# A GpSimd drain ahead of the last scatters, full-height products for PV's last keys, and two standing x buffers

## The chip, the cores and the metric

The kernel runs on one NeuronCore of a Trainium2 chip. Its five engines each take instructions from a queue of their own, in order: TensorE (PE, with its weight loads as PEld), VectorE (DVE), ScalarE (ACT), GpSimd (POOL) and SyncE (SP), which mostly issues DMAs. GpSimd issues DMAs too, those whose rows are picked by an index. The metric is the device time of one execution in microseconds, the median of several runs.

## The reference

Three layers run one after the other, on 4 batches of 576 tokens and 512 features.

```
scores = q k^T / 8 - (cum_i - cum_j), causal;  cum = cumsum(max(s, 0))     8 heads of 64
x  = softmax(scores) v                                                     [4, 576, 512]
x  = (sigmoid(conv5(x)) * (x @ w_val)) @ w_out                             gated convolution
e  = the expert of each token: argmax(x @ w_gate) if local gate < 0.5, else the previous token's
out = softmax(x @ w_gate)[e] * relu(x @ w1[e]) @ w2[e]                     8 experts, 1024 wide
```

All inputs and outputs are float32.

## The kernel before

The first part of the program is the attention and the convolution layer, the second the experts.

Attention goes over 16 pairs of heads (`attention(p)`, 4 pairs for each batch). A pair's queries are cut into tiles of 128 and a rest of 64. For each tile PE makes the scores (L648, L653), where the bias comes in as one more product with gate rows `G`; DVE adds the mask and takes the row minimum (L680, L693), ACT takes the exponential (L701), POOL scales by the reciprocal sum (L725), PE transposes the result through a unit matrix (L737) and ACT or DVE copy it to the buffers `PT0` and `PT1` (L747 to L762). The 576 keys are four blocks of 128 and a last block of 64. The last block is transposed for both heads of the pair by L739 and copied by L755 into 64 partitions of `PT1`.

PV (`pv`, L789) then multiplies by v. It works on two halves of the queries: half 0 has 256 columns and keys 0 to 255, half 1 has 320 columns and all keys. The two heads lie side by side in the array, 64 columns each. The step for the last 64 keys (`j == 4`) takes its v from the tile `rv`, 64 partitions, loaded once for each batch by `last64`, and has K = 64. ACT copies the result into a tile `x` (L799) with four zero columns in front (L797, written on POOL), which the five taps of the convolution read (DVE, L814 and L816) and which POOL splits into a high and a low part (L803, L807). There are two x buffers; the first use of one is the s input.

What sets the order: every piece of work in the first part is a step with an engine, an estimated cost, what it waits for and a rank, and `Plan.order` simulates the engines and writes the instructions in the order that comes out. Buffers are taken into account as slots. A step's instructions are all issued where the step stands. POOL's first steps are constants: the unit matrix, `gr_set`, `zeros` (L290), the masks, small ones and blanks. `bias_rows` makes the gate rows `gr` from s: DVE scans, POOL multiplies (L390), and SP writes them to DRAM as `gates` (L407). `bias_in` loads each pair's `G` (L590), the first pair's straight from `gr`.

The experts come in a loop (`ffn`), in the order of their load. `up(e)` makes the hidden layer (L1375 to L1382), `turn` transposes gathered token rows for the next expert, `down(e, h)` makes the output (L1549), and POOL scatters each block of rows to the output in DRAM (L1458). The last expert's last block is made and scattered in two halves (`down_end`, L1516 to L1526). POOL's gathers and scatters wait in its queue for their indices and rows. At the end all engines meet (L1663): SP waits for every landing, each engine executes DRAINs, and the semaphores are cleared.

The loop that the last part of the change touches is

```
for e in range(E):
    if 0 < e < E - 1:
        tokens(e + 1)
    h = up(e) if e else up_first()
    if e + 1 < E:
        turn(e + 1, 0)
        turn(e + 1, 1)
    down(e, h)
```

Of the kernel before, what the change touches and what calls it, by code (L numbers as in the profile page):

```python
# [8 lines left out]
F32 = mybir.dt.float32  # L9
# [11 lines left out]
B, H, S, D = 4, 8, 576, 64  # L21
# [154 lines left out]
def build(tc, q, k, v, s, w_val, conv_w, w_out, w_gate, w_local, w1, w2, out, dbg=None):  # L176
    nc = tc.nc
    with ExitStack() as ctx:
# [75 lines left out]
        HL = {"q": (1, 0, -0.125), "k": (2, 3, 1.0)}  # L254


        PT0 = ap_.tile([P, 2, 384], F32, name="PT0")
        PT1 = ap_.tile([P, 2, 4 * 320 + P], F32, name="PT1")
        ready = {}
# [19 lines left out]
        def constants():  # L279
# [8 lines left out]
                                            channel_multiplier=1)  # L288

            def zeros():  # L290
                for g in G:
                    nc.gpsimd.memset(fv(g), 0.0)
                for t in QK:
                    nc.gpsimd.memset(fv(t[0:64, 0:2, 576:640]), 0.0)
                    nc.gpsimd.memset(fv(t[64:P, 0:2, 512:576]), 0.0)
# [51 lines left out]
        def bias_rows():  # L347

            plan.rank = -8
            ss, sg, s1, sc = slot("x"), slot("gr"), slot("g"), slot("g")
            tl = {}

            def s_zero():
                tl["s"] = new(mp, "x", "s_sb", [48, S])
                nc.vector.memset(tl["s"], 0.0)

            def one_set():
                tl["one"] = new(mp, "g", "one", [48, S])  # L360
                nc.vector.memset(tl["one"], 1.0)

            def gr_set():
                gr = tl["gr"] = new(ap_, "gr", "gr", [48, 4, 2, 640], F32R)
                nc.gpsimd.memset(fv(gr[:, 0::2, 0]), 1.0)
                nc.gpsimd.memset(fv(gr[:, 1::2, 1]), 1.0)
                nc.gpsimd.memset(fv(gr[:, 0::2, 1, 576:640]), 0.0)
                nc.gpsimd.memset(fv(gr[0:16, :, 0, 576:640]), 0.0)
                nc.gpsimd.memset(fv(gr[32:48, :, 0, 512:576]), 0.0)

            def scan():
                s_sb, cum = tl["s"], new(mp, "g", "cum", [48, S])
                tl["cum"] = cum
                nc.vector.tensor_scalar(s_sb, s_sb, 0.0, None, ALU.max)
                nc.vector.tensor_tensor_scan(cum, tl["one"], s_sb, 0.0, ALU.mult, ALU.add)

            def keys(z):
                gr, cum = tl["gr"], tl["cum"]
                if z == 0:
                    nc.vector.tensor_scalar(gr[:, 0, 1, 0:S], cum, -1.0, None, ALU.mult)  # L380
                else:
                    nc.vector.scalar_tensor_tensor(gr[:, 2, 1, 0:S], cum, -1.0, fv(gr[:, 0, 1, 0:S]), ALU.mult,
                                                   ALU.subtract)

            def queries(z, on_pool):
                gr = tl["gr"]
                for a, e, i, o, n in ((0, 48, 0, 0, 512), (0, 16, 512, 512, 64), (32, 48, 512, 576, 64)):
                    src, dst = fv(gr[a:e, 2 * z, 1, i:i + n]), gr[a:e, 2 * z + 1, 0, o:o + n]
                    if on_pool:
                        nc.gpsimd.tensor_scalar(dst, src, -1.0, 1.0, ALU.mult, ALU.mult)  # L390
                    else:
                        nc.scalar.activation(dst, src, AF.Copy, scale=-1.0)

            a = add("DVE", 0.6, s_zero, on=[ss])
            d = [add("SP", 0.1, lambda h=h: nc.sync.dma_start(
                out=tl["s"][32 * h:32 * h + 16], in_=s.rearrange("b (p two) s -> two (b p) s", two=2)[h]), a, on=[ss],
                lat=FAR) for h in range(2)]
            o = add("DVE", 0.6, one_set, on=[s1])
            w = ready["gr_set"] = add("Pool", 2.6, gr_set, on=[sg])
            c = add("DVE", 1.1, scan, d, o, on=[ss, s1, sc])  # L400
            k, r = None, []
            for z in range(2):
                k = add("DVE", 0.68 if z else 0.4, lambda z=z: keys(z), c, w, k, on=[sc, sg])
                p = R["qP"] > z
                r.append(add(*(("Pool", 1.0) if p else ("ACT", 0.95)), lambda z=z, p=p: queries(z, p), k, on=[sg]))
            ready["gr"], ready["gr_slot"] = (tl, r), sg
            ready["gates"] = [add("SP", 0.91, lambda h=h: nc.sync.dma_start(  # L407
                out=gates[:, h].rearrange("p r k s -> p (r k) s"),
                in_=fv(tl["gr"][32 * h:32 * h + 16]).rearrange("p r k s -> p (r k) s")), r, on=[sg], rank=0.2, lat=FAR)
                for h in range(2)]  # L410
# [80 lines left out]
        def load(p, nm):  # L491
# [19 lines left out]
            if p % NP == 0:  # L511
                sr = rest[b, nm, "slot"] = slot("r" + nm)

                def last64():
                    t = rest[b, nm] = new(ap_, "r" + nm, f"r{nm}_{b}", [64, H, D])
                    nc.sync.dma_start(out=t, in_=src[b, :, 512:576].rearrange("h p d -> p h d"))
                rest[b, nm, "step"] = add("SP", 0.28, last64, on=[sr], lat=FAR)
            return steps, sn
# [79 lines left out]
        def attention(p):  # L598
# [121 lines left out]
            def weigh(u, i, ss, st_, r):  # L720
# [13 lines left out]
                def turn():  # L734
                    ps = tl["pt"] = ps_t.tile([P, 4, P], F32, tag="t", name=f"t_{p}_{u}")
                    for j in range(min(t + 1, 4)):
                        nc.tensor.transpose(ps[:, j], tl["tt"][:, P * j:P * j + P], ident)  # L737
                    if fifth:
                        nc.tensor.transpose(ps[0:64, 1], last4["tl"]["tt"][:, 512:576], ident)  # L739

                def far(h, c, w, n):
                    return PT1[:, h, 0:1280].rearrange("p (j s) -> p j s", s=320)[:, 0:n, c:c + w]
# [9 lines left out]
                        nc.scalar.activation(far(0, 256, 64, 4), ps[:, :, 0:64], AF.Copy)  # L752

                def ev5():
                    nc.scalar.activation(PT1[0:64, :, 1344:1408], tl["pt"][0:64, 1].rearrange("j (h i) -> j h i", h=2),  # L755
                                         AF.Copy)
                half = 0 if t < 2 else 1
                a = add("PE", 0.107 * (min(t + 1, 4) + fifth), turn, n, last4["n"] if fifth else None,
# [18 lines left out]
            def pv(half):  # L777
                tl["ps", half] = ps_s.tile([P, 512], F32, tag="s", name=f"pv_{p}_{half}")
                vt, vr = nat[p]["v"], rest[b, "v"]
                for j in range(5) if half else range(2):  # L780
                    K = P if j < 4 else 64
                    if half:
                        c = (0, 0, 0, P, 256)[j]
                        o = 320 * j + c if j < 4 else 1344
# [2 lines left out]
                        c, o, w = P * j, 2 * P * j, 256 - P * j  # L787
                    for h in range(2):
                        nc.tensor.matmul(tl["ps", half][64 * h:64 * h + 64, c:c + w],  # L789
                                         lhsT=vt[0:K, j, h] if j < 4 else vr[:, 2 * hp + h],  # L790
                                         rhs=(PT1 if half else PT0)[0:K, h, o:o + w], start=j == 0,
                                         stop=j == (4 if half else 1))

            def x_out(half):
                if "x" not in tl:
                    tl["x"] = new(mp, "x", f"x_{p}", [P, 4 + S])
                    nc.gpsimd.memset(tl["x"][:, 0:4], 0.0)  # L797
                w = 320 if half else 256
                nc.scalar.activation(tl["x"][:, 4 + 256 * half:4 + 256 * half + w], tl["ps", half][:, 0:w], AF.Copy)  # L799

# [510 lines left out]
        def ffn():  # L1311
# [261 lines left out]
            for e in range(E):  # L1573
# [3 lines left out]
                if e + 1 < E:  # L1577
                    turn(e + 1, 0)
                    turn(e + 1, 1)
                down(e, h)  # L1580


# [85 lines left out]
```

## Time and profile before

| | |
|---|---|
| median of 3 runs | 619.11 us (618.69 to 619.46) |
| profiled execution | 616.59 us, its span 614.8 us |
| mean granted clock of TensorE | 0.984 |
| PE busy | 577.8 us, 4346 matmuls |
| DVE busy | 410.5 us |
| ACT busy | 339.4 us |
| POOL busy | 243.7 us |
| attention and convolution | about the first 315 us |
| first and last PV product (L789) | 37.1 and 313.7 us |

The profile shows one execution. Its span runs from the first to the last instruction; the execution's own time has 1.8 us more around that. A busy share is an average over stages with different limits, so the stretches have to be looked at one by one. In the rows below, the times of a timeline's row are its start, its length, and in brackets how long the engine stood idle before it and what ended that. A q behind an engine's name (POOLq, SPq) is its queue's own instructions, which don't count as busy. A drain is one of these.

### The profile page before, as it was taken

Reading aid. Unit: us, or ns where it says so; the run is one execution under the profiler, and the core shown is the slowest. Engines: PE = TensorE matmul, PEld = TensorE weight load, DVE = VectorE, ACT = ScalarE, POOL = GpSimd, SP = SyncE. Lnnn points to the kernel's source line nnn. Section 1 sums busy time; section 2 is a strip of 40 time slices with the busy share of each in tenths; the row PEclk is TensorE's granted clock in tenths of the full one; section 3 lists DMA queues with packets and bytes.
Section 4 is the critical chain, followed back from the end, with each engine's and each line's share of the span. In section 5 each row is a group of like instructions: output and inputs, shape, how many; then the busy total and the mean of one; then the engine's idle time right before and its main releaser. Section 6 shows DMA issues by size and latency. Waiting matters only on the chain. (4 is left out here: it accounts for less than half of the span.)

```text
span 614.8 us, 12466 instructions
## 1 busy us (share of the span) xinstructions
PE 577.8 (94%) x4346; PEld 503.3 (82%) x4346; DVE 410.5 (67%) x1029; ACT 339.4 (55%) x869; POOL 243.7 (40%) x377
## 2 busy tenths in 40 slices
PE   5899989999899988999989989999999999999994
PEld 4677678778777887777979987898998999999894
DVE  5589999968887668886699356455353636465550
ACT  2669868787478953677334325544243536355440
POOL 8367868553543433464550344030404004033101
PEclk8989999999999998999999999999999999999997
DMA  7734322322132310210133725273645537365710
GB/s 163 130 92 144 91 81 77 86 55 64 46 87 64 81 47 27 63 28 29 26 125 136 139 59 164 79 245 111 196 171 171 190 107 253 104 244 171 263 47 29
DMA packets 82838, 68.96 MB, mean 112 GB/s; under 512 B 60557, under 2 KB 66829, under 8 KB 82740
## 3 DMA queue, kind: packets, MB, share of 16 engines
q1 hardware_dynamic: 78788, 58.24, 33.2%
q0 software_dynamic: 3984, 9.88, 4.8%
q8 instruction: 36, 0.59, 0.4%
q14 instruction: 30, 0.25, 0.2%
HBM read 57.90 MB, written 10.79 MB: 112 GB/s over the span
## 5 line engine op out<-in xcount | busy, mean ns | idle before, releaser
L725 POOL TENSOR_SCALAR tt<-tt,st 128x512 f32<-128x512 f32 (+2 forms) x144 | 93.0, 661 | 103.0 <-DVE st L714 52.0
L1308 DVE TENSOR_TENSOR wl<-raw,wh 128x1024 fp32r<-128x1024 f32 x64 | 78.3, 1224 | 34.2 <-ACT wh L1305 33.8
L701 ACT ACTIVATE tt<-tt,st 128x384 f32<-128x384 f32 (+3 forms) x144 | 83.2, 583 | 12.4 <-DVE st L680 8.6
L1375 PE MATMUL h<-xth,wh 128*128 128x256 f32 (+5 forms) x256 | 73.7, 306 | 1.4 <-DVE xtl L1115 1.4
L1375 PE MATMUL h<-xth,wl 128*128 128x256 f32 (+5 forms) x256 | 72.9, 302 | 0.0
L680 DVE CUSTOM_DVE_ANT_0 tt<-s,mask 128x512 f32<-128x512 f32 (+3 forms) x128 | 57.9, 483 | 13.9 <-PE s L653 7.5
L1458 POOL DMA_INDIRECT out_dram<-out,id x21 | 28.6, 1362 | 96.7 <-ACT out L1456 83.3
L1305 ACT ACTIVATE wh<-raw 128x1024 fp32r<-128x1024 f32 x64 | 66.5, 1052 | 0.3 <-DMA raw<-in_moe_w_dram 0.3
L816 DVE SCALAR_TENSOR_TENSOR g<-x,cw,g 128x576 f32<-128x576 f32 x64 | 64.8, 1012 | 0.7
L737 PE MATMUL t<-ident,tt 128*128 128x128 f32 x384 | 61.9, 283 | 3.5 <-POOL tt L725 2.2
L1381 ACT ACTIVATE hh<-h 128x256 fp32r<-128x256 f32 (+5 forms) x64 | 27.1, 425 | 58.5 <-PE h L1375 52.1
L1382 DVE SCALAR_TENSOR_TENSOR hl<-h,hh 128x256 fp32r<-128x256 f32 (+5 forms) x64 | 29.8, 469 | 43.4 <-ACT hh L1381 43.4
L737 PEld LDWEIGHTS t<-ident,tt 128*128 128x128 f32 x384 | 43.3, 142 | 15.7 <-POOL tt L725 8.1
L1340 POOL DMA_INDIRECT xg<-x2d,id x20 | 20.9, 1046 | 87.2 <-DMA id<-ids 59.2
L929 PE MATMUL x<-wo_h,yl 128*128 128x266 f32 (+3 forms) x144 | 43.2, 300 | 7.8 <-DVE y L874 2.9
L653 PE MATMUL s<-QK 64*128 64x256 f32 (+2 forms) x384 | 48.9, 356 | 1.2 <-DVE st L693 1.2
L1375 PEld LDWEIGHTS h<-xth,wh 128*128 128x128 f32 x256 | 48.3, 189 | 1.9 <-DVE xtl L1115 1.6
L1375 PEld LDWEIGHTS h<-xth,wl 128*128 128x128 f32 x256 | 48.4, 189 | 0.2
L789 PE MATMUL pv<-PT,nv 128*64 128x320 f32 (+3 forms) x384 | 47.3, 386 | 0.0
L1375 PE MATMUL h<-xtl,wh 128*128 128x256 f32 (+5 forms) x256 | 46.3, 302 | 0.0
L929 PE MATMUL x<-wo_h,yh 128*128 128x266 f32 (+3 forms) x144 | 41.6, 289 | 0.0
L929 PE MATMUL x<-wo_l,yh 128*128 128x266 f32 (+3 forms) x144 | 41.6, 289 | 0.0
(269 smaller groups left out, 1499.4 us busy)
## 6 DMA issues: line engine op xcount, KB each, us to landing
raw<-in_moe_w_dram SPq DMA_DIRECT2D x64, 512.0 KB
nv<-in_v_dram SPq DMA_DIRECT2D x32, 128.0 KB
x2d<-x SPq DMA_DIRECT2D x32, 128.0 KB
nk<-in_k_dram SPq DMA_DIRECT2D x26, 128.0 KB
nq<-in_q_dram SPq DMA_DIRECT2D x26, 128.0 KB
wsc<-in_moe_w_val_dram SPq DMA_DIRECT2D x4, 512.0 KB
wsc<-in_moe_w_out_dram SPq DMA_DIRECT2D x4, 512.0 KB
nk<-in_k_dram SPq DMA_DIRECT2D x3, 256.0 KB
```

What stands on the lines that cost most here:

```text
L653: nc.tensor.matmul(ps[hh][:, 0:N], lhsT=q[:, P * t:P * t + P], rhs=k[:, 0:N], start=n == 0, stop=n == 3)
L680: nc.vector.tensor_tensor_reduce(out=tl["tt"][:, 0:W], in0=ps[h][:, 0:W], in1=mask[:, 512 - W:512], scale=1.0, scalar=3.0e38, op0=ALU.add, ...
L701: nc.scalar.activation(tt[:, 0:W], tt[:, 0:W], AF.Exp, bias=st[:, 0, i:i + 1], scale=-1.0, accum_out=st[:, 1, i:i + 1])
L725: nc.gpsimd.tensor_scalar(tl["tt"][:, 0:W], tl["tt"][:, 0:W], st_["st"][:, 2, i:i + 1], 1.0, ALU.mult, ALU.mult)
L737: nc.tensor.transpose(ps[:, j], tl["tt"][:, P * j:P * j + P], ident)
L789: nc.tensor.matmul(tl["ps", half][64 * h:64 * h + 64, c:c + w], lhsT=vt[0:K, j, h] if j < 4 else vr[:, 2 * hp + h], rhs=(PT1 if half else ...
L816: nc.vector.scalar_tensor_tensor(tl["g"], x[:, t:t + S], cw[:, hp, t:t + 1], tl["g"], ALU.mult, ALU.add)
L929: nc.tensor.matmul(ps[0:m, 0:c1 - c0], lhsT=yy[:, kc] if both else yy[:, kc, P * t:P * t + m], rhs=wt_[:, kc, c0:c1], start=n == 0, stop=n ...
L1305: nc.scalar.activation(hi, raw, AF.Copy)
L1308: nc.vector.tensor_tensor(lo, raw, fv(hi), ALU.subtract)
L1375: nc.tensor.matmul(ps[:, 0:N], lhsT=w[:, P * f:P * f + P], rhs=xx[:, kc, c], start=n == 0, stop=n == 11)
L1382: nc.vector.scalar_tensor_tensor(hl[:, c], ps[:, 0:N], 0.0, fv(hh[:, c]), ALU.max, ALU.subtract)
```

## The change

Four things are edited.

1. In the last expert, between `up` and `down`, POOL gets a `drain`.
2. The tile for the last 64 keys of v becomes `VR`, one standing tile with 128 partitions. The keys lie in partitions 64 to 127, the partitions 0 to 63 are set to zero once. L739 turns columns 448 to 575 of the last tile, where it had 512 to 575, so that 128 rows come out; the 64 ahead meet the zero rows. The copy to `PT1` is of 128 partitions, and all steps of PV have K = 128.
3. The x buffers are two standing tiles `X`. Their four zero columns are written once, in `zeros`, and the memset in `x_out` is gone.
4. `zeros` writes these two pads and VR's zero rows ahead of G and QK. Its planned cost stays the same, and so does the order of all other steps.

```
+        X = [mp.tile([P, 4 + S], F32, name=f"X{n}") for n in range(SIZES["x"])]
+        VR = ap_.tile([P, H, D], F32, name="VR")
...
             def zeros():
+                for x in X:
+                    nc.gpsimd.memset(x[:, 0:4], 0.0)
+                nc.gpsimd.memset(VR[0:64], 0.0)
                 for g in G:
                     nc.gpsimd.memset(fv(g), 0.0)
...
             def s_zero():
-                tl["s"] = new(mp, "x", "s_sb", [48, S])
+                tl["s"] = X[0][0:48, 4:4 + S]
...
                 def last64():
-                    t = rest[b, nm] = new(ap_, "r" + nm, f"r{nm}_{b}", [64, H, D])
+                    if nm == "v":
+                        rest[b, nm] = VR
+                        t = VR[64:P]
+                    else:
+                        t = rest[b, nm] = new(ap_, "r" + nm, f"r{nm}_{b}", [64, H, D])
...
                     if fifth:
-                        nc.tensor.transpose(ps[0:64, 1], last4["tl"]["tt"][:, 512:576], ident)
+                        nc.tensor.transpose(ps[:, 1], last4["tl"]["tt"][:, 448:576], ident)
...
                 def ev5():
-                    nc.scalar.activation(PT1[0:64, :, 1344:1408], tl["pt"][0:64, 1].rearrange("j (h i) -> j h i", h=2),
+                    nc.scalar.activation(PT1[:, :, 1344:1408], tl["pt"][:, 1].rearrange("j (h i) -> j h i", h=2),
                                          AF.Copy)
...
-                    K = P if j < 4 else 64
...
                         nc.tensor.matmul(tl["ps", half][64 * h:64 * h + 64, c:c + w],
-                                         lhsT=vt[0:K, j, h] if j < 4 else vr[:, 2 * hp + h],
-                                         rhs=(PT1 if half else PT0)[0:K, h, o:o + w], start=j == 0,
+                                         lhsT=vt[:, j, h] if j < 4 else vr[:, 2 * hp + h],
+                                         rhs=(PT1 if half else PT0)[:, h, o:o + w], start=j == 0,
                                          stop=j == (4 if half else 1))
...
             def x_out(half):
-                if "x" not in tl:
-                    tl["x"] = new(mp, "x", f"x_{p}", [P, 4 + S])
-                    nc.gpsimd.memset(tl["x"][:, 0:4], 0.0)
+                tl["x"] = X[(p + 1) % len(X)]
...
                 if e + 1 < E:
                     turn(e + 1, 0)
                     turn(e + 1, 1)
+                else:
+                    nc.gpsimd.drain()
                 down(e, h)
```

How the instructions stand now is shown at two places. The first is POOL's queue at the start of the program, from the last memsets of the gate rows `gr` to the mask, as it was before:

```order
L369 MEMSET gr 16x4x64
L292 MEMSET G_102 128x1280
L292 MEMSET G_103 128x1280
L294 MEMSET QK_104 64x2x64
L295 MEMSET QK_104 64x2x64
L294 MEMSET QK_105 64x2x64
L295 MEMSET QK_105 64x2x64
L281 MEMSET mask 128x512
```

And the same place of the changed kernel:

```order
L374 MEMSET gr 16x4x64
L294 MEMSET X_106 128x4
L294 MEMSET X_107 128x4
L295 MEMSET VR 64x512
L297 MEMSET G_102 128x1280
L297 MEMSET G_103 128x1280
L299 MEMSET QK_104 64x2x64
L300 MEMSET QK_104 64x2x64
L299 MEMSET QK_105 64x2x64
L300 MEMSET QK_105 64x2x64
L283 MEMSET mask 128x512
```

Three memsets have come in ahead of G; everything behind stands as it did.

The second is PE's queue at the PV of pair 0, where `nv` holds v's first 512 keys and `rv` or `VR` the last 64. Before:

```order
L789 MATMUL pv_0_627<-PT_106,nv_196 64x256 x2
L789 MATMUL pv_0_627<-PT_106,nv_196 64x128 x2
L789 MATMUL pv_1_637<-PT_107,nv_196 64x320 x6
L789 MATMUL pv_1_637<-PT_107,nv_196 64x192 x2
L789 MATMUL pv_1_637<-PT_107,rv_216 64x64 x2
L648 MATMUL s_4_1_658<-QK_105 128x288 x3
```

And in the changed kernel:

```order
L797 MATMUL pv_0_631<-PT_109,nv_198 64x256 x2
L797 MATMUL pv_0_631<-PT_109,nv_198 64x128 x2
L797 MATMUL pv_1_641<-PT_110,nv_198 64x320 x6
L797 MATMUL pv_1_641<-PT_110,nv_198 64x192 x2
L797 MATMUL pv_1_641<-PT_110,VR 64x64 x2
L657 MATMUL s_4_1_660<-QK_105 128x288 x3
```

No instruction of PE has moved; the last step reads another tile, with 128 rows. On POOL the 16 memsets of the x tiles are gone from their places. The drain is not listed in such rows; it stands behind the scatters of expert 6.

## Rows read from the trace of the kernel before

**Rows 1.** The page: busy us, share of the span, instructions.

```profile
PE 577.8 (94%) x4346; PEld 503.3 (82%) x4346; DVE 410.5 (67%) x1029; ACT 339.4 (55%) x869; POOL 243.7 (40%) x377
```

**Rows 2.** Stretches: length, busy us of the five engines, clock, DMA share, GB/s.

```profile
80.00:120.00 40.00, 38.68 (x331) 30.69 (x330) 38.90 (x110) 29.41 (x92) 27.26 (x34) 1.00 0.35 90
240.00:280.00 40.00, 39.35 (x319) 30.59 (x320) 30.89 (x96) 26.24 (x80) 19.96 (x33) 0.96 0.19 48
```

**Rows 3.** Instructions of L1663: ns min/median/max, first and last start us.

```profile
L1663 POOLq DRAIN  x3: 46/103/5462, 608.5 to 614.5; - x3
L1663 SPq DRAIN  x3: 7/7/13, 609.7 to 614.2; - x3
```

**Rows 4.** Timeline of POOL, the last expert's scatters.

```profile
601.27 0.98 POOL L1458 DMA_INDIRECT out_dram<-out,id  x1 [15.88 <-ACT out L1456]
...
606.80 0.98 POOL L1526 DMA_INDIRECT out_dram<-out,halves  x1 [1.81 <-POOLq L1223]
```

**Rows 5.** DMA issues of POOL's queue: count, median us to landing.

```profile
xg<-x2d,id POOLq DMA_INDIRECT x22, 3.7
out_dram<-out,id POOLq DMA_INDIRECT x21, 5.8
ids<-tokp,place POOLq DMA_INDIRECT x20, 4.4
```

**Rows 6.** Instructions of L1652, the program's start.

```profile
L1652 POOLq DRAIN  x1: 186/186/186, 0.3 to 0.3; - x1
```

**Rows 7.** Timeline of POOL, 4 to 15 us.

```profile
4.34 2.27 POOL L292 MEMSET G<- 128x1280 f32 x2
...
7.52 0.53 POOL L281 MEMSET mask<- 128x512 f32 x1
...
12.96 1.64 POOL L390 TENSOR_SCALAR gr<-gr 48x512 fp32r<-48x512 f32 x3
```

**Rows 8.** Timeline of SP's queue and of PE, gate rows of pairs 0 and 1.

```profile
16.10 1.45 SPq L590 DMA_DIRECT2D G<-gr  x2
...
27.19 0.87 SPq L590 DMA_DIRECT2D G<-gates  x2
...
30.74 0.77 PE L653 MATMUL s<-G 64*128 64x512 f32 x2 [2.25 <-DMA G<-gates]
```

**Rows 9.** Timeline of PE in three instants: what runs then, pair 15's PV.

```profile
313.16 0.50 PE L789 MATMUL pv<-PT,nv 128*64 128x192 f32 x4
...
313.32 0.33 PE L789 MATMUL pv<-PT,nv 128*64 128x192 f32 x2
313.58 0.27 PE L789 MATMUL pv<-PT,rv 64*64 64x64 f32 x2
...
313.69 0.22 PE L789 MATMUL pv<-PT,rv 64*64 64x64 f32 x2
313.85 0.39 PE L929 MATMUL x<-wo_h,yl 128*128 128x266 f32 x1
```

**Rows 10.** Instructions that read rv, and idle time ahead of them (us, times).

```profile
L789 PE MATMUL pv<-PT,rv x64: 218/242/268, 39.9 to 313.7; 64*64 64x64 f32 x64
...
  issue: 3.3, 12
```

**Rows 11.** Instructions of L739 and L737.

```profile
L739 PE MATMUL t<-ident,tt x16: 271/272/273, 35.5 to 307.6; 128*64 128x128 f32 x16
...
L737 PE MATMUL t<-ident,tt x384: 270/273/469, 24.8 to 309.2; 128*128 128x128 f32 x192
```

**Rows 12.** Instructions of L797, and who waited for them (us, times).

```profile
L797 POOL MEMSET x<- x16: 93/98/422, 36.2 to 311.5; 128x4 f32 x16
...
  PEld t L737: 0.2, 1
```

**Rows 13.** Timeline of PE at 238.89.

```profile
238.89 0.39 PE L929 MATMUL x<-wo_h,yl 128*128 128x266 f32 x1 [2.93 <-DVE y L874]
```

**Rows 14.** The stretch behind it, columns as in group 2.

```profile
239.80:243.00 3.20, 3.20 (x16) 3.20 (x16) 2.63 (x7) 0.87 (x2) 0.31 (x1) 0.50 0.11 39
```

## The prediction

> **What bounds the kernel now.** I read the page's busy shares first: TensorE (PE) is busy 94% of a span of 614.8 us [rows 1]. Then I cut the attention part into stretches. From 240 to 280 us PE is busy 39.35 of 40 us and leads alone; from 80 to 120 us VectorE (DVE) is as full as PE, 38.90 against 38.68 of 40 us [rows 2]. So microseconds taken from PE count in full in the later stretches, and only in part where DVE is level with it. Last I read the two ends, where PE isn't the bound. The instructions of the program's last line show what fills the end: GpSimd (POOL) executes three DRAINs of 46, 103 and 5462 ns, the first from 608.5 us on; SyncE (SP), which collects all landings, starts its own at 609.7 [rows 3]. So from about 609.8 to 614.0 the chip waits for one POOL instruction, 4.2 us. At the front POOL works through its constants without a pause, and the gate rows of the first attention pair wait for it [rows 7, 8].
>
> **The drain.** The new instruction stands on POOL behind the scatters of expert 6 and ahead of those of the last expert, the first of which starts at 601.27 after 15.88 us idle [rows 4]. A drain of even 5.5 us lies wholly inside that, and nothing but that scatter is queued behind it. What is the last drain worth if an earlier one has done its work? The trace has four POOL drains: 186 ns at the start, ahead of any DMA from this queue [rows 6], then the long one behind some 63 of them (22 + 21 + 20 [rows 5]; three others leave the quotient the same within 5%), then the two short ones with none in between. Which of the three in the group is the long one follows from the times: it starts at 608.5, and the last at 614.5. So a drain's length goes with what was issued since the one before. 5462 / 63 is 87 ns per DMA. With a drain near 585 us, three scatters are left for the last one (601.27, one in between, 606.80 [rows 4]): 3 x 87 ns = 0.26 us, or 0.45 with the 186 ns of an empty one. It would end before 609.1, ahead of SP. SP is late next, and the end moves from 614.0 to 609.8: **-4.2 us**. The bounds are 0 (the long time is a fixed price of any DMA since the last drain; 3 cost as much as 66) and -4.2 (SP's row). I take -4.2: the rows at hand range with the work behind them.
>
> **PV's last 64 keys.** PV runs two column halves of 64 side by side, and every product comes as two passes, so a step is two pairs of records. Before, the last step uses 64 rows (64\*64) behind steps of 128 rows (128\*64). At pair 15 the last two 192-column pairs start at 313.16 and 313.32, 0.16 us apart; the 64-row pair behind starts at 313.58, 0.26 later [rows 9]. So 0.10 us go where the shape of the array changes. The weight loads say the same: 3.3 us of "issue" (waiting for nothing that shows) ahead of them in 12 places [rows 10]. With 128 rows there is no change of shape at the entry: 64 products [rows 10] are 16 steps of four, 16 x 0.10 = 1.6 us less. The exit: 0.16 us from the second 64-row pair (313.69) to the next instruction (313.85) [rows 9]. In 7 of the 16 steps, by the order of PE, the next is PV's other half with the shape 128\*64, and 0.16 becomes the 0.11 of unbroken pairs (313.58 to 313.69): 7 x 0.05 = 0.35. Together 1.9 us. Inside the step I leave the spacing at 0.11, the row of this very step; if the wider shape hides the weight loads it could halve, 16 x 0.055 and 7 x 0.055 more, 3.2 in all. The transpose in front (L739) loads 64 columns of weights and gets 128; it takes 272 ns and the 128-wide ones a median of 273 [rows 11]. So it costs nothing, nor does its eviction, which has as many elements in each partition as before.
> How much reaches the end: ten of the 16 steps lie behind 120 us, where PE leads; of the six before I count half, so 13/16 of 1.9, 1.5; I take **-1.4 us**, between -3.2 and 0 (all of it lost in waits for DVE).
>
> **The buffers.** 16 memsets of 128x4 with a median of 98 ns leave POOL, 1.6 us. The list of who waited for them has one entry, PE's weight loads for 0.2 us [rows 12]: **-0.2**, between -1.6 and 0. What replaces them stands at the front, ahead of the G memsets: two of 128x4 and one of 64x512, for which the nearest row is mask's, 128x512 in 0.53 us [rows 7]. With the small ones between 0 (overlapped) and 98 ns each that is 0.53 to 0.73 us. From there POOL has no pause: even the multiplications of gr, which feed the gates, start at 12.96 without an idle time [rows 7], so they end 0.6 later. Queued behind them: SP waits for them with G<-gr at 16.10, and in SP's queue behind that stand nk, both gates stores, nq and the loads G<-gates at 27.19, for which PE stands idle 2.25 us, until 30.74 [rows 8]. PE's first gate products wait for the same. So **+0.6 us**, between 0 (what SP issues in between swallows it) and +0.73.
>
> **The sum.** -4.2 - 1.4 - 0.2 + 0.6 = -5.2 us on the profiled execution's 616.59, so 611.4. The median of the runs is 619.11, 2.5 above that execution; I carry the 2.5 over: 613.9 us.
>
> **Rivals.**
> 1. The drain has a fixed price. Then the new one costs 5.5 us in POOL's idle time and the last one 5.5 again. For it: there is only one long drain in the trace, so "per DMA" and "once" can't be told apart by it. Against it: it runs 4.2 us past the point where SP has seen every landing, so it isn't waiting for data, and what outlasts the data is more likely bookkeeping that grows with the DMAs. It gives -1.0: 618.1.
> 2. The gain on PE is lost in waits for DVE, which is 97% busy from 80 to 120 us and also ends PE's 2.93 us wait at 238.89 [rows 2, 13]. Only the late start, the memsets and the drain stay: -3.8, so 615.3.
> [...]
> 4. Slower. A drain in the middle makes the scatter behind it pay as if POOL started afresh: the scatter of 601.27 takes its 0.98 us and 5.46 more and ends at 607.7, the two behind follow some 1.3 us apart, the third starts at 609.3 instead of 606.80, and the last drain costs its full length. That is +2.5 on rival 1: 620.6. It decides once the first scatter is late by more than the 2 us that it has ahead of the next. Against it: behind the 186 ns drain at the start POOL goes on without such a gap. [...] No row here shows such a gap ahead of a POOL instruction.
>
> **How the numbers follow.** Forecast 613.9: 0.35, with its own range 612.6 to 615.2. Fixed drain 618.1: 0.20. PE's gain lost 615.3: 0.15. Low clock gone 612.3: 0.15; one more 615.5: 0.10. Slower 620.6: 0.05. A measurement of this kernel tells 0.2% (1.24 us) from no change, so faster means under 617.9. All cases but the fixed drain and the slower one lie below that, 0.75, and of the fixed drain's 0.20 two fifths (PV giving more than 1.4): 0.83. Its other three fifths are no change: 0.12. Slower: 0.05. The range runs from 611.2 (the clock case with a little more from PV) to 618.4 (about half of the fixed drain's case).
>
> **What would show it.** Right: the last long DRAIN under 1 us and POOL's next step right behind SP's drain, with a DRAIN of about 5.2 us inside POOL's idle time after 585; the 64-column pair 0.16 us behind the last 192-column pair in all 16 steps, and no "issue" time ahead of its weight loads; gr's multiplications at about 13.6, and PE's wait for the gates ending at about 31.3. Wrong: a last drain that keeps its 5.5 us, or an attention part that ends later than before although its PV steps are shorter.

## The result and the profile after

The changed kernel takes 612.26 us (median of 6 runs, 611.76 to 614.65), the kernel before 619.61 (6 runs, 618.69 to 620.97). The ratio is 0.9889, with a 95% interval of 0.9871 to 0.9907, so 5.8 to 8.0 us less. Ratios and intervals here are those on record; a ratio isn't the quotient of the two medians and differs from it by up to 0.14%. The profiled execution took 612.25 us, its span 610.5.

I read the profile after in the order of the prediction's steps. First the page, against [rows 1]: PE is as busy as before, and POOL has 13 instructions fewer (16 memsets gone, three added).

```profile
PE 577.5 (95%) x4346; PEld 505.6 (83%) x4346; DVE 410.8 (67%) x1029; ACT 339.1 (56%) x869; POOL 248.2 (41%) x364
```

Then the end of the program: the instructions of the meeting of all engines (they were L1663 [rows 3]), of the added drain (L1587) and of POOL's semaphore step ahead of the meeting (L1229). Columns are ns min/median/max, first and last start in us.

```profile
L1671 POOLq DRAIN  x3: 46/109/1929, 607.2 to 610.2; - x3
L1671 SPq DRAIN  x3: 7/7/13, 609.6 to 609.9; - x3
...
L1587 POOLq DRAIN  x1: 6532/6532/6532, 583.7 to 583.7; - x1
...
L1229 POOLq INC_SWDGE_SEM  x1: 271/271/271, 606.9 to 606.9; - x1
```

In the kernel before, the last of these was longer too:

```profile
L1223 POOLq INC_SWDGE_SEM  x1: 1531/1531/1531, 606.9 to 606.9; - x1
```

The long drain now stands at 583.7, in idle time, and the last one is over at 609.1 (607.2 + 1.9), ahead of SP's drain at 609.6. To see what that is worth I take the last product on PE, in the timeline of before and then of after:

```profile
605.73 0.28 PE L1516 MATMUL h<-wh,hh 128*128 128x256 f32 x1
```

```profile
605.36 0.28 PE L1522 MATMUL h<-wh,hh 128*128 128x256 f32 x1
```

From its start to the end of the span it was 9.1 us (614.8 - 605.73) and is 5.1 (610.5 - 605.36): 4.0 us less. Up to the last product the two profiles differ by only 0.4 us, and that is not because little changed there.

PV's last keys, by the instructions of L797 and by the timeline of PE in the same instants of pair 15 as in [rows 9]:

```profile
L797 PEld LDWEIGHTS pv<-PT,VR x64: 137/137/137, 43.0 to 315.0; 128*64 128x64 f32 x64
L797 PE MATMUL pv<-PT,VR x64: 219/220/222, 43.2 to 315.1; 128*64 128x64 f32 x64
...
  issue: 2.0, 10
```

```profile
314.83 0.33 PE L797 MATMUL pv<-PT,nv 128*64 128x192 f32 x2
314.99 0.28 PE L797 MATMUL pv<-PT,VR 128*64 128x64 f32 x4
...
315.04 0.23 PE L797 MATMUL pv<-PT,VR 128*64 128x64 f32 x2
315.20 0.39 PE L935 MATMUL x<-wo_h,yl 128*128 128x266 f32 x1
```

The first pair of the step starts 0.16 us behind the last 192-column pair (it was 0.26), the second 0.05 to 0.06 behind the first (0.11), and the next instruction 0.16 behind that, as before. So the inside of the step is shorter as well. The "issue" time ahead of the weight loads hasn't gone: it is 2.0 us in 10 places, where it was 3.3 in 12.

The front, by the timeline of POOL and of PE, against [rows 7, 8]:

```profile
4.34 0.15 POOL L294 MEMSET X<- 128x4 f32 x2
4.41 0.53 POOL L295 MEMSET VR<- 64x512 f32 x1
4.87 2.28 POOL L297 MEMSET G<- 128x1280 f32 x2
...
14.47 1.98 POOL L395 TENSOR_SCALAR gr<-gr 48x512 fp32r<-48x512 f32 x3
```

```profile
32.19 0.68 PE L662 MATMUL s<-G 64*128 64x512 f32 x2 [1.89 <-DMA G<-gates]
```

G's memsets come 0.53 us later, but gr's multiplications 1.5 (12.96 to 14.47, forecast 13.6), and PE's gate products of pair 1 come 1.45 later (30.74 to 32.19). The rest of the 1.5 lies in POOL instructions that were not touched, half of it in the selects on the mask, before and after:

```profile
8.90 1.19 POOL L287 TENSOR_SCALAR_AFFINE_SELECT mask<-mask 64x64 f32<-64x64 f32 x2
```

```profile
9.30 1.66 POOL L289 TENSOR_SCALAR_AFFINE_SELECT mask<-mask 64x64 f32<-64x64 f32 x2
```

In the ten profiles without the early memsets (those of the experiments included) this pair takes 0.52 to 1.85 us, and gr's multiplications start anywhere from 11.96 to 14.12. Compared at the same length of this pair, gr starts later with the memsets by 0.5 to 0.6 us at 1.66 (13.86 and 13.93, then 14.47), by 0.6 at 1.85 (14.12, then 14.71), by 0.5 to 0.9 at 1.2 (12.96 to 13.32, then 13.83) and by 1.2 at 0.64 (11.96, then 13.18). So the memsets' own part is nearer to 0.6 us than to 1.5.

One difference stood in no step of the prediction. The first tap of the convolution on DVE, before and after:

```profile
L814 DVE TENSOR_SCALAR g<-x,cw x16: 503/675/1856, 40.8 to 317.0; 128x576 f32<-128x576 f32 x16
L814 DVEq EVENT_SEMAPHORE  x9: 21/21/21, 40.7 to 316.9; - x9
```

```profile
L820 DVE TENSOR_SCALAR g<-X,cw x16: 504/521/1553, 44.0 to 318.4; 128x576 f32<-128x576 f32 x16
```

Nine waits of 21 ns are gone from DVE's queue, and the longest tap of before, pair 15's, has gone from 1.86 us to 0.52. The experiment on the x tiles takes that up.

### The profile page after: what moved, and what is told of

Its sections match the earlier page's. It is cut to its first block, busy times and chain, and to the rows that moved or that the text cites. A ratio compares the mean times of both kernels' runs of the same rounds, so it can differ in the third digit from the quotient of the medians.

```text
span 610.5 us, 12445 instructions
## 1 busy us (share of the span) xinstructions
PE 577.5 (95%) x4346; PEld 505.6 (83%) x4346; DVE 410.8 (67%) x1029; ACT 339.1 (56%) x869; POOL 248.2 (41%) x364
## 3 DMA queue, kind: packets, MB, share of 16 engines
q0 software_dynamic: 3984, 9.88, 4.9%
## 4 chain that ended last, share of the span: by engine, by line
PE 71%; DVE 15%; POOL 4%; DMA 4%; issue 3%; ACT 2%; SPq 1%; POOLq 0%; ACTq 0%; DVEq 0%
PE h L1381 16%; PE h L1555 11%; PE x L935 7%; PE h L1484 7%; PE val L874 6%; PE s L662 6%; PE t L746 5%; PE pv L797 5%; DVE g L822 4%; PE s L657 2%; DVE tt L689 2%; DVE yl L898 2%; PE xT L1361 1%; DMA gates<-gr 1%; DMA xg<-x2d,id 1%
## 5 line engine op out<-in xcount | busy, mean ns | idle before, releaser
L689 DVE CUSTOM_DVE_ANT_0 tt<-s,mask 128x512 f32<-128x512 f32 (+3 forms) x128 | 58.0, 484 | 13.6 <-PE s L662 8.7
L822 DVE SCALAR_TENSOR_TENSOR g<-X,cw,g 128x576 f32<-128x576 f32 x64 | 66.0, 1031 | 0.7
L797 PE MATMUL pv<-PT,nv 128*64 128x320 f32 (+3 forms) x384 | 47.5, 390 | 0.0
```

Source lines behind the costliest of these rows:

```text
L689: nc.vector.tensor_tensor_reduce(out=tl["tt"][:, 0:W], in0=ps[h][:, 0:W], in1=mask[:, 512 - W:512], scale=1.0, scalar=3.0e38, op0=ALU.add, ...
L822: nc.vector.scalar_tensor_tensor(tl["g"], x[:, t:t + S], cw[:, hp, t:t + 1], tl["g"], ALU.mult, ALU.add)
```

## The experiments

Two theories stand behind them. **Mine:** each part does its own share, the drain most of it. **The rival:** the drain carries nearly all, and what differs in the attention part is where PE's low clock falls. Each run has the kernel before beside it on the same chip: 618.62 us in the first four, 618.55 in the next four, 619.1 in the last four.

**The drain alone, and the change without it.** The one edit, added to before and taken from after:

```
                     turn(e + 1, 1)
+                else:
+                    nc.gpsimd.drain()
                 down(e, h)
```

> Before plus the drain in the last expert, nothing else. Theory A (the drain works off what has piled up on GpSimd's queue, so the last one has little left): span 3.9 to 4.2 us shorter than before, the final DRAIN ending within 0.3 us of SP's own, everything up to the last product as in before; time -0.6 to -0.7%. Theory B (the drain is a part of the gain only, and the rest of the measured 1.1% comes from the attention part): the same -0.65% here, and the no-drain kernel keeps -0.3 to -0.5%. Rival (the drain carries the whole gain in the timed runs): -1.0 to -1.1% here.

Measured: 614.7 us, 0.9923 (0.9899 to 0.9948): 4.8 us less by the ratio, 3.9 by the medians. The rival's 1.0 to 1.1% lies at the edge of the interval. The engines' meeting in its profile, and its last product:

```profile
L1665 POOLq DRAIN  x3: 46/109/2038, 610.5 to 613.5; - x3
```

```profile
608.96 0.28 PE L1516 MATMUL h<-wh,hh 128*128 128x256 f32 x1
```

From that product to the end of the span (613.8) it is 4.9 us, where it was 9.1: 4.2 us less, as forecast. The product itself comes 3.2 us later than before; that is the low clock, which the last of the experiments takes up.

> The changed kernel without the drain. Theory A/B: the final DRAIN is back at about 5.5 us; the PV steps save 3.0 us by their spacing, the late start and the low clock behind it cost 1.8 to 3.3 us, so the time is between -0.4% and +0.1% of before. Rival (drain carries the whole gain): within 0.1% of before.

Measured: 616.34 us, 0.9961 (0.9931 to 0.9991), -2.3 us, and the last DRAIN takes 5.46 us again. The two together give the whole: the drain is about two thirds, and the rest is more than nothing.

**What the drain's length goes with.** One drain in expert 1 instead of the last, then one in every expert:

```
                     turn(e + 1, 1)
+                if e == 1:
+                    nc.gpsimd.drain()
                 down(e, h)
```

> Before with one drain in expert 1 instead of the last one: some 33 of POOL's 66 DMAs stand behind it. Per-DMA theory: the last DRAIN takes 33 x 83 = 2.7 us, the early one as much (or till its scatters land), and the program's end comes 1.5 to 2.7 us earlier behind the last product than before. Fixed-price theory: the last DRAIN takes 5.5 us as before. Any-drain theory (an earlier drain switches something once and for all): under 2 us, ending with the last landing.

The meeting of the engines in this run, and POOL's step ahead of it:

```profile
L1665 POOLq DRAIN  x3: 46/103/2748, 607.5 to 610.8; - x3
...
L1223 POOLq INC_SWDGE_SEM  x1: 871/871/871, 606.6 to 606.6; - x1
```

33 of POOL's 66 DMAs are issued behind the early drain here. The last DRAIN is 5462 ns for 66 and 2748 for 33: 82.8 and 83.3 ns for each, no fixed price. Packets would not give that: 2368 of the queue's 3984 lie behind the early drain, 59% and not half. The step ahead of it goes the same way, 1531, 871 and 271 ns for 66, 33 and 3 DMAs: 20 ns for each and 0.2 us. The last product starts at 605.45 and the span ends at 611.1, 5.65 us later, 3.4 less than before, which is 33 x 103 ns. That is beyond my 1.5 to 2.7, because I had left the second instruction out. The early drain itself takes 9.09 us. (This kernel was timed once, 612.92 us; the reading rests on its rows.) In the changed kernel the added drain agrees: the scatter in front of it is issued from 583.97 on and takes 0.98 us, and from there to the drain's end it is 5.3 us, 84 ns for each of its 63 DMAs.

> Before with a POOL drain in every expert, between up and down: eight drains more. Per-DMA theory: each is as long as its DMAs since the one before, at 84 ns: about 2.3 us for the first (27 DMAs), 0.5 us for the six behind (6 or so each), or as long as the last of these needs to land; the last DRAIN of the program ends with the last landing as with one early drain. Fixed-price theory: each takes over 5 us. Ratio by the first 0.992 (as the single drain), by the second above 0.995, since POOL's gathers wait behind the drains.

Measured: 614.86 us, 0.9925 (0.99 to 0.9951), as with the single drain. The eight drains take 4.5 to 9.2 us each, though few DMAs lie between them:

```profile
L1580 POOLq DRAIN  x8: 4478/6384/9167, 383.4 to 587.6; - x8
```

They end 0.6 to 1.6 us behind the last packet of the queue's DMAs ahead of them (with 2 to 6 DMAs since the drain before, 0.6 to 1.0; with 27, 1.6). So these drains outlasted the landing of the scatters ahead of them by that much, and their length doesn't tell the price by DMA; my 0.5 us was the wrong one of the two lengths I gave. The time shows no cost of the seven drains more.

**PV alone, and PV with half the height.** In the first, VR's zero rows are written behind gr's multiplications, and the x tiles stay as before.

```
+                if z:
+                    nc.gpsimd.memset(VR[0:64], 0.0)
...
-                                         lhsT=vt[0:K, j, h] if j < 4 else vr[:, 2 * hp + h],
+                                         lhsT=vt[:, j, h] if j < 4 else vr[:, 2 * hp + h],
```

> The full-height PV step alone: VR's zero rows are written behind gr's last multiplication, x tiles and their 16 memsets as in before, no drain. Theory (PV saves 3.0 us and the front costs nothing when the memsets stand behind gr): -0.3 to -0.5%, the 16 steps with the spacing of the changed kernel. Rival (what PV saves is lost in waits for DVE): within 0.1% of before though the steps are shorter.

Measured: 618.12 us, 1.0001 (0.9977 to 1.0025): nothing, although each step is as short in its trace as in the changed kernel's. I come back to that below.

The second keeps all tiles, transposes and copies of the change but multiplies partitions 64 to 127 alone:

```
-                                         lhsT=vt[:, j, h] if j < 4 else vr[:, 2 * hp + h],
-                                         rhs=(PT1 if half else PT0)[:, h, o:o + w], start=j == 0,
+                                         lhsT=vt[:, j, h] if j < 4 else vr[64:P, 2 * hp + h],
+                                         rhs=(PT1 if half else PT0)[0 if j < 4 else 64:P, h, o:o + w], start=j == 0,
```

> The change without the drain, pads late, but PV's last step multiplies only partitions 64 to 127 of VR and of PT1: the same tiles, transposes and evictions, half the height. Shape theory: the spacing of before comes back, the entry 0.26 us, the second pair 0.11 us behind the first, and weight loads of 131 ns instead of 137. Rival (another tile, another place of the step): 0.16 and 0.06 as with 128 rows.

```profile
L798 PEld LDWEIGHTS pv<-PT,VR x64: 129/130/133, 41.1 to 315.9; 64*64 64x64 f32 x64
L798 PE MATMUL pv<-PT,VR x64: 218/242/267, 41.1 to 315.9; 64*64 64x64 f32 x64
```

The kernel was timed once, 617.8 us. The spacing of before is back: 0.26 us at the entry, 0.11 inside. So the height of the product sets it, not the tile.

**The x tiles alone.** Standing tiles, pads written once behind gr's multiplications, the rest as before:

```
+                if z:
+                    for x in X:
+                        nc.gpsimd.memset(x[:, 0:4], 0.0)
...
-                if "x" not in tl:
-                    tl["x"] = new(mp, "x", f"x_{p}", [P, 4 + S])
-                    nc.gpsimd.memset(tl["x"][:, 0:4], 0.0)
+                tl["x"] = X[(p + 1) % len(X)]
```

> Before with the two standing x tiles alone, their pads written once behind gr's multiplications; PV, drain and front as before. Theory A (the standing x tiles carry what the change without its drain gained over the PV part alone, 0.9961 against 1.0001): ratio 0.996, -2.4 us. Theory B (16 memsets of 98 ns off POOL, for which PE waited 0.2 us in all): ratio 0.9993 to 1.000, -0.4 to 0 us, and the PV part alone was timed too high or lost its gain to the clock.

Measured: 617.81 us, 0.9981 (0.9956 to 1.0005). Both expectations lie in the interval, but the trace shows what the tiles do. Pair 15, before, then with the standing tiles; rows of POOL, DVE and PE from the timeline:

```profile
316.96 0.67 POOL L803 TENSOR_SCALAR xh<-x 128x576 fp32r<-128x576 f32 x1 [5.32 <-ACT x L799]
316.98 1.86 DVE L814 TENSOR_SCALAR g<-x,cw 128x576 f32<-128x576 f32 x1 [1.15 <-ACT x L799]
317.58 0.95 POOL L1271 MEMSET xg<- 128x1024 f32 x1
...
319.38 0.34 PE L929 MATMUL x<-wo_h,yl 128*64 128x266 f32 x1 [2.28 <-ACT x L935]
```

```profile
321.17 0.52 DVE L816 TENSOR_SCALAR g<-X,cw 128x576 f32<-128x576 f32 x1 [1.08 <-ACT X L801]
321.22 0.99 POOL L805 TENSOR_SCALAR xh<-X 128x576 fp32r<-128x576 f32 x1 [5.36 <-ACT X L801]
322.16 0.95 POOL L1273 MEMSET xg<- 128x1024 f32 x1
...
322.24 0.34 PE L931 MATMUL x<-wo_h,yl 128*64 128x266 f32 x1 [0.90 <-ACT x L937]
```

POOL and DVE wait for the same ACT copy. Before, DVE had to wait for POOL's memset of the pad too. That was done at 311.6 us, 5.2 before the ACT copy ended, but an EVENT_SEMAPHORE of 21 ns stands ahead of the tap in DVE's queue (the last of the nine, at 316.9), which I take for that second wait, and DVE came 0.02 us behind POOL. (DVE starts 0.10 us behind the end of the ACT copy with the wait and 0.03 without it, POOL 0.09 in both profiles.) Its tap then lasted 1.86 us, over POOL's two instructions of 0.67 and 0.95, and PE waited 2.28 us at the end of the chain DVE, ACT, PE. With the standing tiles the nine are gone, DVE is 0.05 us ahead of POOL, the tap takes 0.52, and POOL's instruction takes longer instead (0.67 becomes 0.99). PE's wait is 1.38 us shorter. So 1.34 us of the tap's length go with which of the two starts first, by 0.02 or 0.05 us; the mechanism was not shown. It is no chance of one execution: pair 15's tap takes 1.86 us in all six profiles without standing tiles and 0.52 in all eight with them. The 16 taps together take 13.08 us before and 9.96 here (9.93 to 10.37 in the eight). No run takes the wait away and leaves the memsets, so that the wait did it rests on these rows.

**PV and the x tiles, no drain, zeros late.**

> The whole change without the drain, pads and zero rows written late: PV's full height and the standing x tiles alone. Theory A (x tiles carry the gain): the same as the x tiles alone, 0.996. Theory B (PV's shape carries it, 3.0 us off PE of which 1.5 to 2.5 reach the end): 0.996 to 0.9975 and 1.5 to 2.5 us below the x tiles alone. Theory C (both are lost in waits for DVE): within 0.1% of before.

Measured: 615.92 us, 0.9963 (0.993 to 0.9996), -2.3 us: more than the x tiles alone, as the theory of PV's shape has it, but the intervals overlap.

**The three memsets alone.**

```
                 for g in G:
+                    nc.gpsimd.memset(fv(g[:, 0, 0:4]), 0.0)
+                nc.gpsimd.memset(fv(G[1][0:64, 0, 0:512]), 0.0)
+                for g in G:
                     nc.gpsimd.memset(fv(g), 0.0)
```

> Before with nothing but three memsets more at the front, of the sizes that the change has there (two of 128x4, one of 64x512), ahead of G's and into G's own tiles. Front theory: gr's multiplications, the gates and PE's first products come 0.6 to 1.5 us later and that stays to the end: ratio 1.001 to 1.0025. Rival (later waits swallow it): 1.000. At an equal clock the attention part should end 0.6 to 1.5 us behind that of before; each low-clock stretch behind 20 us more or less moves that by 1.7 us.

Measured: 618.91 us, 1.0009 (0.9985 to 1.0033). gr's multiplications start at 14.71 and the gate products at 32.44, as late as in the changed kernel. The interval holds both expectations.

**The whole change with the zeros behind gr's multiplications** (`zeros` left as it was, the memsets in the step that makes the queries' rows), and later once more beside the whole change:

```
+                if z:
+                    for x in X:
+                        nc.gpsimd.memset(x[:, 0:4], 0.0)
+                    nc.gpsimd.memset(VR[0:64], 0.0)
```

> The whole change, but the pads and VR's zero rows are written behind gr's last multiplication instead of ahead of G. Theory (the three memsets delay the gates): gr's first multiplication back at about 13.0 us, PE's first gate product at 18.7, and the time 0.1 to 0.3% below the changed kernel. Rival (the late start came from the input loads of that execution, not from the memsets): gr's multiplications early, but no difference in time to the changed kernel.

Measured: 613.01 us, 0.9895 (0.9847 to 0.9943), no lower than the whole change's 0.9889. gr's multiplications start at 13.93 and the first gate product at 20.02, not at 13.0 and 18.7: I had taken the profile before for the usual one.

> The whole change with the pads and VR's zero rows written behind gr's multiplications, second time, now on the same chip as the whole change itself. Theory front: the three early memsets cost 0.6 to 1.5 us at the gates, so this is 0.6 to 1.5 us below the whole change (ratio to before 0.986 to 0.988). Rival: later waits swallow that; then the two agree within 0.3 us.

> The whole change once more, beside the other kernels of this call. If its parts add up as they were timed alone (drain alone 0.9923, the rest without the drain 0.9961), the ratio is 0.988 to 0.989, 611.5 us where before gives 618.6. Its profile is the second of this kernel. Theory A (where PE falls to the low clock is set by the program): the same stretches as in the first, at 9.6, 33.5 and 166.6 us. Theory B (it differs between executions): at least one of the stretches behind 20 us at another place, with steps of 1 to 3 us in PE's lead at these places and nowhere else.

Measured: 611.24 us, 0.9869 (0.9828 to 0.9911) with late zeros; 612.51 us, 0.989 (0.9845 to 0.9935) for the whole change. The late version is 1.3 us lower, as the front theory has it, and its two ratios average 0.9882 against 0.989 for the change; the intervals don't part them. The low clock stood at other places in the second profile of the same kernel (at 20.9 and 242.7 us too, where the first has none), so the low clock is not set by the program alone, as theory B has it.

**The clock, taken out.** In two profiles with the attention code of before, the stretches at the lower clock differ. These are the drain in expert 1 and then the drain alone, over the same three slices (columns as in [rows 2]):

```profile
20.00:60.00 40.00, 36.07 (x313) 27.06 (x313) 32.01 (x109) 30.11 (x96) 22.59 (x31) 0.96 0.54 125
150.00:180.00 30.00, 27.38 (x221) 22.26 (x219) 25.62 (x59) 15.59 (x44) 14.44 (x20) 1.00 0.21 56
```

```profile
20.00:60.00 40.00, 36.24 (x292) 26.92 (x292) 30.70 (x103) 28.43 (x89) 21.69 (x30) 0.91 0.51 117
150.00:180.00 30.00, 27.37 (x201) 22.53 (x201) 26.39 (x60) 16.01 (x47) 13.87 (x17) 0.94 0.21 55
```

0.91 for 0.96 of 40 us and 0.94 for 1.00 of 30 us are two stretches more at a granted clock of 0.50 in the second, 6.8 us, and so, as an estimate by that share, some 3.4 us of full clock lost. So I note for each profile the start of the first expert's first transposes back on PE (`h<-ident,h_rows`), where the attention part is over, take off half of the time that PE spent at the lower clock between 25 and 385 us, and compare:

| kernel | start, us | low clock, us | start less half of it |
|---|---|---|---|
| before | 390.8 | 6.8 | 387.4 |
| drain in expert 1 | 390.5 | 6.8 | 387.1 |
| drain alone | 394.0 | 13.6 | 387.2 |
| drain in every expert | 394.3 | 13.6 | 387.5 |
| three memsets alone | 395.8 | 13.6 | 389.0 |
| x tiles alone | 393.2 | 13.6 | 386.4 |
| x tiles, PV at 64 rows | 391.7 | 10.2 | 386.6 |
| PV alone | 392.2 | 14.9 | 384.7 |
| PV and x tiles | 389.3 | 10.2 | 384.2 |
| whole change, zeros late | 388.9, 391.9 | 10.2, 17.0 | 383.8, 383.4 |
| whole change without drain | 390.0 | 10.2 | 384.9 |
| whole change | 390.4, 391.1 | 10.2, 10.2 | 385.3, 386.0 |

The four kernels with before's attention code come within 0.4 us of each other (mean 387.3), though their starts lie 3.8 us apart: the correction holds to that here. At PV's last product, worked out the same way, the same four still lie 1.0 us apart (310.3 to 311.3), so what one profile alone shows is no surer than about 1 us. By the table the x tiles are worth 0.7 to 0.9 us, PV's height 2.6 alone and 2.7 on top of the x tiles (three profiles with a mean of 383.8 against 386.5), and the early memsets cost 1.6 (385.4 against 383.8) to 1.7. PV alone is the least sure of these: 1.3 us of its 14.9 belong to a stretch that began at 19.5 us, and another stretch falls where DVE is as full as PE and half of it may be too much to take off:

```profile
77.50:80.90 3.40, 3.40 (x18) 2.95 (x17) 3.36 (x6) 2.42 (x6) 3.32 (x4) 0.51 0.00 0
```

The timed runs can be put at an equal clock too, since each has its mean granted clock on record. Over the 74 runs of the kernel before beside the experiments, a straight line falls by 3.4 us for each 0.01 of clock. With the line of the runs timed together alone the figures below move by up to 0.3 us. Off the line lie, as mean and 95% interval of the mean of 12 runs each: PV alone -2.0 us (0.6 either way), the x tiles alone -0.7 (0.7), PV and x tiles -2.5 (0.9), the whole change without the drain -2.6 (0.5), the three memsets alone +0.8 (1.0).

## Why the prediction came out right

Forecast 613.9, measured 612.26, inside the range and on the forecast side. Step by step:

- **The drain, -4.2: right, in size and in mechanism.** 4.0 us less behind the last product in this pair of profiles and 4.2 with the drain alone (and up to 4.5 beside the standing x tiles, whose kernels without the drain have 9.4 us there; why, no run shows), and the price goes by DMA (83 ns, where I had 87 from 63 DMAs; the trace has 66). What is late next is SP, as forecast. Two details were wrong: the last DRAIN takes 1.93 us, not under 1, and it ends just behind the landing of the last rows (in the four profiles of the drain alone, the eight drains and the whole change it takes 1.71 to 2.04 us and ends 0.5 to 0.6 behind the queue's last packet each time); and a second instruction with a price by DMA stands ahead of it, which I had not looked for. Rival 1 (fixed price) is out by the run with the drain in expert 1. The slower rival is out by the profile after: the first scatter behind the drain, at 600.90, takes 0.98 us and the last starts at 606.43 (and before, POOL's longest idle time that shows no cause is 0.4 us).
- **PV, 1.9 us on PE: mis-sized.** The entry gives 0.10 in every step, as worked out (in one, at 87.7 us, the records interleave). But I left the spacing inside at 0.11, "the row of this very step", and it halved: the row was one of the shape that goes, not of the shape that comes. With 0.10 and 0.05 in 16 steps, and 0.10 more in the 7 with PV's other half behind, it is 3.1 us, near my other bound of 3.2. At an equal clock 2.0 of them (0.6 either way) reach the end by the runs and 2.6 to 2.7 by the profiles, where I had taken 1.4 (a little under the 1.5 that my own sum gave). The eviction behind the transpose, which I had at no cost, takes ACT a median of 284 ns (L764) where it took 264 (L755). That the gain is lost in waits for DVE (rival 2) is not what happens. The sign "no issue time" did not come.
- **The buffers, -0.2: mis-sized, and for another reason than I weighed.** I priced the memsets by who waited for them as POOL's work. By the rows of pair 15 their cost was in the wait that they put on DVE. It is 1.38 us at one place, of which 0.7 to 0.9 arrives by the profiles, and 0.7 (0.7 either way) by the runs.
- **The front, +0.6: about right at gr; what reaches the end is open.** The memsets take what I reckoned (0.53 us later at G, in most comparisons 0.5 to 0.9 at gr where the select on the mask took as long), yet the gate products come 1.45 us later in this pair of profiles, because the select and others took longer too. Over all profiles, the four with these memsets have the products start at 32.19, 32.46, 32.44 and 31.20 (mean 32.07), the ten without at 29.96 to 32.13 (mean 31.32): 0.75 us, my upper bound. With the memsets alone, against the four profiles of before's attention code (mean 31.34), it is 1.1 there, 1.4 at PV's first product and 1.5 at its last, at an equal clock: what is lost is lost at the front, and next to nothing behind it. The profiles' 1.6 to 1.7 at the end is more than the runs bear out: +0.8 (1.0 either way) for the memsets alone, and no difference between the change without the drain with early and with late zeros (-2.6 and -2.5).
- **The sum.** From the profiles, -4.0, -2.3, -0.8 and +1.6 are -5.5; I had -5.2. The gains in the attention part were too small in my sum. By the runs at an equal clock the change without the drain is -2.6, and with 4.2 for the drain that is -6.8; the two ratios of the whole change, 0.9889 and 0.989, are -6.9 and -6.8 (by the medians -7.4 and -6.0). So my sum is 1.6 short, in PV and the x tiles. No run shows the 1.6 us by which the two clock cases, 612.3 and 615.5, lie off the forecast; the traces show a granted clock of 1.00 or 0.50, and of 0.50 from 239.7 to 243.1 us of the kernel before. That the measured 612.26 is just that 612.3 is chance: that stretch is gone from the profile after, but in all it has 10.2 us of low clock in the attention part, more than the 6.8 before.
- **The median above the profile, 2.5 us: right to carry over.** The profile before had 6.8 us of low clock in the attention part, where most others have 10.2 or more; its 616.59 was one of the kernel's shorter executions (615.49 to 621.76 among 29).

**What stays open.** PV alone gains 2.0 us at an equal clock and nothing in its 12 runs as they are. The mean granted clock over these runs is 0.976, over the 29 of before beside them 0.981. Six of those 29 have 0.976, and they took 620.1 to 621.8 us; the eight runs of PV alone between 0.970 and 0.978 took 617.4 to 621.1. Its profile has low stretches at 77.5 and 319.9 us, which no other profile has. So its gain went into the clock, as far as these runs go; why this kernel meets the low clock more often than the same PV with standing x tiles (0.981) was not found.

## What to carry to other kernels

Price a memset, a copy or any small producer also by the wait that it leaves at its reader: here the pad's memset went with 21 ns more in DVE's queue, and where two engines started on the same event, 0.02 us behind or 0.05 ahead went with a tap of 1.86 or of 0.52 us. Put a drain of GpSimd's queue into the last long idle time of that engine if it issues many DMAs: here the one at the end then came after 3 of them instead of 66 and took 1.93 us instead of 5.46. Where a change replaces a shape, take its price from rows of the new shape, and before two profiles are compared, take the low-clock time out of both and see how far profiles of the same code still lie apart.

## What the runs showed of the hardware

- GpSimd's DRAIN at the end took 83 ns for each DMA of its queue since the last drain (5462 ns for 66, 2748 for 33); with 3 it took 1.71 to 2.04 us and ended 0.5 to 0.6 behind the queue's last packet. Its INC_SWDGE_SEM took 0.2 us and 20 ns for each (1531, 871 and 271 ns for 66, 33 and 3). In the middle of work, with 2 to 33 DMAs since the last drain, a DRAIN took 4.5 to 9.2 us and ended 0.6 to 1.9 us behind the queue's last packet.
- Behind 128\*64 products, a 64\*64 pair of 64 columns came 0.26 us after the one ahead and 0.11 after its like; a 128\*64 pair of the same columns 0.16 and 0.06. A 128\*64 product behind came 0.16 us after the 64\*64 pair and 0.06 after the 128\*64 one (seven steps). So 0.10 us went with the change of shape at the entry and again at that exit; the mechanism was not shown.
- Pair 15's DVE tap took 1.86 us in six profiles, starting 0.02 us behind a POOL instruction in the kernel before, and 0.52 in eight, starting 0.05 us ahead of it with the x tiles alone and in the changed kernel.
- POOL's two selects on the mask took from 0.52 to 1.85 us at the same place of POOL's queue.
